# Summing pairs of tap products by an accumulating DMA ahead of TensorE's transposes

## The chip, the cores and the metric

The kernel runs on one NeuronCore of a Trainium2 chip. The metric is the time of one execution on the device, in microseconds (us). A ratio given below is the mean time of one kernel's fast runs over that of the other's fast runs of the same rounds, so it is not quite the ratio of the medians quoted beside it.

## The reference

A dynamic convolution (softmax over seven tap weights per token and head, then a weighted sum of seven shifted rows) feeds a two-layer product with `h - tanh(h)` between the layers.

```
w = exp(weight_gen - max); w = w / (sum(w) + 1e-9)        # (8, 4096, 8 heads, 7 taps)
conv[s, h, :] = sum_k w[s, h, k] * x_pad[s + k, h, :]     # 192 channels = 8 heads x 24
h = conv @ w_in                                           # (32768, 192) @ (192, 2048)
out = (h - tanh(h)) @ w_out                               # (32768, 2048) @ (2048, 192)
```

## The kernel before

The tokens go through in 32 superblocks of 1024. For each, GpSimd multiplies x by the weights, once per tap (seven `prod` tiles, tokens on partitions). TensorE then transposes each product by a matmul against an identity and adds the seven taps up in PSUM in the same step (`pc`): 3 chunks x 4 column blocks x 2 row halves x 7 taps = 168 small matmuls. ScalarE copies the sum to `convT`. Sixteen first products (`ph`, one per f tile of 128) follow, each read by ScalarE (`th`, tanh) and then VectorE (`gt`, the difference); the second product (`po`) of the superblock before is woven in.

```python
psum_h = ctx.enter_context(tc.tile_pool(name="psum_h", bufs=3, space=bass.MemoryType.PSUM))
# ... products(n): GpSimd, seven products, each in its own buffer (two of each)
for k in range(K):
    prod = ppool.tile([P, NC, J, H, GC], BF16, name=f"prod{k}", tag=f"prod{k}")
    eng = nc.vector if k in on_vector else nc.gpsimd
    eng.tensor_mul(prod[:]..., x_t[:, k : k + J, :]..., wsm[:, :, :, k : k + 1]...)
# ... conv(n, chunks): TensorE
pc = psum_h.tile([P, 2, HT], FP32, name="pc", tag="ph")      # shares the three ph buffers
for k in range(K):
    for ci, c in enumerate(chunks):
        for j in range(JH):
            for r in range(2):
                nc.tensor.matmul(pc[:, r, col : col + R], lhsT=prods[k][...], rhs=ident[...], ...)
# ... the main loop
for n in range(NTOT):
    if n + 2 < NTOT:
        products(n + 2)
    for p in range(J):
        gemm1(n, 2 * p)          # ph, th, gt
        gemm1(n, 2 * p + 1)
        if n >= 1:
            gemm2((n - 1) * J + p)
        if n + 1 < NTOT:
            if p == (2 if n else 5):
                conv(n + 1, (0, 1))      # "first place": 112 matmuls
            if p == (5 if n else 6):
                conv(n + 1, (2,))        # "third chunk": 56 matmuls
```

The softmax here doesn't subtract the row's maximum and nothing guards it: scores larger than these inputs give would overflow.

## Time and profile before

| | before |
|---|---|
| median of 3 runs | 821.86 us (821.55 to 822.88) |
| profiled span | 820.7 us |
| transposes of superblock 2 start | 69.1 us |
| clean superblock in the middle | 23.82 us |
| transposes of superblock 31 start | 767.3 us |

The first line of the page is where a reader starts; it gives busy time, share of the span and number of instructions of each engine:

```profile
PE 769.5 (94%) x16640; PEld 602.6 (73%) x16640; DVE 661.0 (81%) x591; ACT 640.1 (78%) x865; POOL 669.0 (82%) x265
```

It says "TensorE bound". Two lines of the waits give the engine that waited, for what, us in total, times, and the longest:

```profile
PE pc L169 <- issue: 2.6, 5, 1.0
PE po L223 <- issue: 2.4, 3, 1.9
```

These are gaps that no wait in the profile explains. They fall in some of the superblocks; the irregular ones take 24.0 to 24.5 us in the middle of the run. The transposes of superblock 2 are this row of the timeline of 24 to 72 us:

```profile
69.14 1.81 PE L169 MATMUL pc<-ident,prod 64*128 64x64 bf16 x110
```

### The profile page before, as it was taken

The page shows a single profiled execution, that of the slowest core. Times are in us where ns is not written, and L with a number is a line of the kernel's source. Part 1 is how long each engine was busy: PE and PEld are TensorE (multiplying, and loading weights), DVE is VectorE, ACT ScalarE, POOL GpSimd, SP SyncE. Part 2 cuts the span into 40 slices and gives each one's busy share as a digit, 9 for nine tenths or more (in the row PEclk, how much of TensorE's full clock was granted, in tenths as well). Part 3 has the DMA queues.
Part 4 walks back from the last instruction along what each step waited for, and adds up shares of the span by engine and source line. Part 5 has one row for each costly group of instructions (what it writes and reads, how often), then busy time and mean ns, then how long its engine had stood idle before and what let it go on. Part 6 is the DMA issues. An engine that isn't in the chain of part 4 may idle for free.

```text
span 820.7 us, 35994 instructions
## 1 busy us (share of the span) xinstructions
PE 769.5 (94%) x16640; PEld 602.6 (73%) x16640; DVE 661.0 (81%) x591; ACT 640.1 (78%) x865; POOL 669.0 (82%) x265
## 2 busy tenths in 40 slices
PE   0379999999999999999999999999999999999997
PEld 0247777777778777777777777777777878777777
DVE  3987878888888887887888888888888888787783
ACT  0277778888888878888888888888888888888883
POOL 5999999998898888899888889988888898885000
PEclk9989999999999999999999999999999999999999
DMA  8823333233224323332333332233233223301112
GB/s 145 216 80 81 119 120 119 71 119 120 96 77 119 120 70 120 102 94 95 119 102 87 120 120 73 99 119 114 76 120 110 95 87 120 108 3 42 41 41 79
DMA packets 17286, 81.21 MB, mean 99 GB/s; under 512 B 4160, under 2 KB 8816, under 8 KB 12984
## 3 DMA queue, kind: packets, MB, share of 16 engines
q1 hardware_dynamic: 14560, 77.34, 28.2%
q0 software_dynamic: 2576, 1.57, 1.7%
q8 instruction: 130, 2.13, 1.1%
q14 instruction: 20, 0.16, 0.1%
HBM read 54.49 MB, written 25.17 MB: 97 GB/s over the span
## 4 chain that ended last, share of the span: by engine, by line
PE 79%; DVE 13%; ACT 4%; issue 2%; DMA 1%; SPq 0%; POOL 0%; ACTq 0%; DVEq 0%; POOLq 0%
PE ph L192 36%; PE po L223 35%; DVE gt L203 10%; PE pc L169 6%; ACT th L201 4%; DVE prod L146 3%; DMA x_t<-in_x_dram 1%; PE po L264 1%; DVE zr L129 0%; DVE zsum L125 0%; POOL wsm L136 0%; SPq L96 0%; ACT e_t L115 0%; SPq L100 0%; SPq L77 0%
## 5 line engine op out<-in xcount | busy, mean ns | idle before, releaser
L203 DVE TENSOR_TENSOR gt<-ph,th 128x1024 bf16<-128x1024 f32 x512 | 602.5, 1219 | 130.0 <-ACT th L201 130.0
L146 POOL TENSOR_TENSOR prod<-x_t,wsm 128x1536 bf16<-128x1536 f32 x218 | 632.6, 2939 | 78.0 <-issue 70.3
L201 ACT ACTIVATE th<-ph 128x1024 f32<-128x1024 f32 x512 | 496.9, 1022 | 58.3 <-PE ph L192 56.3
L192 PE MATMUL ph<-convT,w_in 64*128 64x512 bf16 x3072 | 393.1, 378 | 13.8 <-DVE gt L203 10.5
L223 PEld LDWEIGHTS <-gt 64*128 64x128 bf16 x7936 | 346.1, 94 | 54.4 <-issue 3.4
L223 PE MATMUL po<-w_out,gt 64*128 64x192 bf16 x7936 | 375.8, 243 | 4.2 <-issue 2.4
L192 PEld LDWEIGHTS <-w_in 64*128 64x128 bf16 x3072 | 171.3, 94 | 128.5 <-issue 38.1
L169 PE MATMUL pc<-ident,prod 64*128 64x64 bf16 x5376 | 93.7, 192 | 29.4 <-POOL prod L146 25.9
L169 PEld LDWEIGHTS <-prod 64*128 64x128 bf16 x5376 | 89.8, 96 | 31.2 <-POOL prod L146 26.2
L179 ACT ACTIVATE convT<-pc 128x1024 bf16<-128x1024 f32 x64 | 51.9, 810 | 65.0 <-PE pc L169 65.0
L248 ACT ACTIVATE out_sb<-po 128x192 f32<-128x192 f32 x248 | 82.5, 333 | 24.3 <-PE po L223 20.7
L115 ACT ACTIVATE e_t<-wg_t 128x448 f32<-128x448 f32 x32 | 18.5, 577 | 20.9 <-DMA wg_t<-in_weight_gen_dram 20.9
L136 POOL TENSOR_TENSOR wsm<-e_t,zr 128x448 f32<-128x448 f32 x32 | 31.1, 972 | 1.7 <-DVE zr L129 1.7
L146 DVE TENSOR_TENSOR prod<-x_t,wsm 128x1536 bf16<-128x1536 f32 x6 | 21.0, 3556 | 10.8 <-DMA x_t<-in_x_dram 9.6
L125 DVE TENSOR_REDUCE zsum<-e_t 128x64 f32<-128x448 f32 x32 | 19.5, 609 | 2.8 <-ACT e_t L115 2.8
L129 DVE RECIPROCAL zr<-zsum 128x64 f32<-128x64 f32 x32 | 17.7, 553 | 3.4 <-DVE zsum L125 0.5
L264 PE MATMUL po<-w_out,gt 64*128 64x192 bf16 x256 | 11.0, 243 | 0.0
L264 PEld LDWEIGHTS <-gt 64*128 64x128 bf16 x256 | 10.8, 93 | 0.0
L276 DVE TENSOR_TENSOR out_sb<-po,ot 128x192 f32<-128x192 f32 x8 | 2.9, 357 | 8.9 <-ACT ot L275 8.9
L275 ACT ACTIVATE ot<-po 128x192 f32<-128x192 f32 x8 | 2.6, 330 | 7.9 <-PE po L264 7.9
L292 POOL DMA_DIRECT2D w_in<-in_moe_w_in_dram x8 | 4.8, 604 | 0.4 <-issue 0.4
L115 ACT ACT_TABLE_LOAD x1 | 1.3, 1283 | 0.7 <-PEq L346 0.7
(8 smaller groups left out, 2.4 us busy)
## 6 DMA issues: line engine op xcount, KB each, us to landing
x_t<-in_x_dram SPq DMA_DIRECT2D x24, 1344.0 KB
out_dram<-out_sb SPq DMA_DIRECT2D x31, 768.0 KB
x_t<-in_x_dram SPq DMA_DIRECT2D x8, 1176.0 KB
wg_t<-in_weight_gen_dram SPq DMA_DIRECT2D x32, 224.0 KB
x_t<-in_x_dram SPq DMA_DIRECT2D x8, 157.5 KB
w_in<-in_moe_w_in_dram POOLq DMA_DIRECT2D x8, 96.0 KB, 11.2
w_in<-w_in SPq DMA_DIRECT2D x1, 768.0 KB
w_out<-in_moe_w_out_dram POOLq DMA_DIRECT2D x1, 768.0 KB, 13.0
```

The source lines that it names most:

```text
L115: nc.scalar.activation(out=e_t[:].rearrange("p j h k -> p (j h k)"), in_=wg_t[:].rearrange("p j h k -> p (j h k)"), func=ACT.Exp,)
L125: nc.vector.reduce_sum(out=zsum[:], in_=e_t[:].rearrange("p j h k -> p (j h) k"), axis=AX.X)
L136: nc.gpsimd.tensor_mul(wsm[:].rearrange("p j h k -> p (j h) k"), e_t[:].rearrange("p j h k -> p (j h) k"), zr[:].rearrange("p (n o) -> p n ...
L146: eng.tensor_mul(prod[:].rearrange("p c j h g -> p j h c g"), x_t[:, k : k + J, :].rearrange("p j (h c g) -> p j h c g", h=H, c=NC), wsm[: ...
L169: nc.tensor.matmul(pc[:, r, col : col + R], lhsT=prods[k][r * R : (r + 1) * R, c, 2 * j : 2 * j + 2].rearrange("p j h g -> p (j h g)"), rh ...
L179: nc.scalar.activation(out=convT[:, c0 : c0 + nch, :].rearrange("p c (j r t) -> p r (c j) t", r=2, t=R), in_=pc[:, :, 0 : nch * JH * R].re ...
L192: nc.tensor.matmul(ph[:, r, :], lhsT=w_in[r * R : (r + 1) * R, c, f * P : (f + 1) * P], rhs=convT[r * R : (r + 1) * R, c, :], start=(c == ...
L201: last_act[0] = nc.scalar.activation(out=th[:], in_=ph_f, func=ACT.Tanh)
L203: nc.vector.tensor_sub(gt[:], ph_f, th[:])
L223: mm = nc.tensor.matmul(po[:, 0:D], lhsT=g_of[n][f][r * R : (r + 1) * R, col : col + P], rhs=w_out[r * R : (r + 1) * R, f, :], start=(r == ...
L248: last_act[0] = nc.scalar.activation(out=out_sb[:, j, :], in_=po[:, 0:D], func=ACT.Copy)
L264: nc.tensor.matmul(po[:, r, 0:D], lhsT=g_of[n][f][r * R : (r + 1) * R, col : col + P], rhs=w_out[r * R : (r + 1) * R, f, :], start=(f == 0 ...
```

## The change

The even taps 0, 2, 4 go into one tile, the odd taps 1, 3, 5 into another, tap 6 into a third. One DMA per superblock adds the odd tile into the even one, so that TensorE has four groups to transpose in place of seven (96 matmuls in place of 168).

```diff
-        prods = []
+        even = ppool.tile([P, NPAIR, NC, J, H, GC], BF16, name="even")
+        odd = ppool.tile([P, NPAIR, NC, J, H, GC], BF16, name="odd")
+        last = ppool.tile([P, NC, J, H, GC], BF16, name="last")
+        dst = {}          # taps 0 to 6: even, odd, even, odd, even, odd, last   (cut)
         for k in range(K):
-            prod = ppool.tile([P, NC, J, H, GC], BF16, name=f"prod{k}", tag=f"prod{k}")
             eng = nc.vector if k in on_vector else nc.gpsimd
             eng.tensor_mul(
-                prod[:].rearrange("p c j h g -> p j h c g"),
+                dst[k].rearrange("p c j h g -> p j h c g"),
                 # ... cut
             )
+            if k == K - 2:
+                nc.gpsimd.dma_start(
+                    out=even[:].rearrange("p i c j h g -> p (i c j h g)"),
+                    in_=odd[:].rearrange("p i c j h g -> p (i c j h g)"),
+                    accum_op=mybir.AluOpType.add,
+                    max_dma_last_dim=3072,
+                )
-        prods_of[n] = prods
+        prods_of[n] = [even[:, i] for i in range(NPAIR)] + [last[:]]
 # ... in conv
-        for k in range(K):
+        for k in range(NPAIR + 1):
```

More of the change, by code (lines that the diff above doesn't have):

```diff
@@ L44 @@
     GC = G // NC
+    NPAIR = K // 2
     assert S % TOK == 0 and D % R == 0 and H * GC == R and F % P == 0
@@ L140, in products @@
         )
-        prods = []
+        even = ppool.tile([P, NPAIR, NC, J, H, GC], BF16, name="even")
+        odd = ppool.tile([P, NPAIR, NC, J, H, GC], BF16, name="odd")
+        last = ppool.tile([P, NC, J, H, GC], BF16, name="last")
+        dst = {}
+        for i in range(NPAIR):
+            dst[2 * i] = even[:, i]
+            dst[2 * i + 1] = odd[:, i]
+        dst[K - 1] = last[:]
         for k in range(K):
-            prod = ppool.tile([P, NC, J, H, GC], BF16, name=f"prod{k}", tag=f"prod{k}")
             eng = nc.vector if k in on_vector else nc.gpsimd
             eng.tensor_mul(
-                prod[:].rearrange("p c j h g -> p j h c g"),
+                dst[k].rearrange("p c j h g -> p j h c g"),
                 x_t[:, k : k + J, :].rearrange("p j (h c g) -> p j h c g", h=H, c=NC),
@@ L152, in products @@
             )
-            prods.append(prod)
-        prods_of[n] = prods
+            if k == K - 2:
[6 more added lines that the diff above has]
+        prods_of[n] = [even[:, i] for i in range(NPAIR)] + [last[:]]
     def conv(n, chunks):
@@ L175, in conv @@
                             start=(k == 0 and ci == 0 and j == 0),
-                            stop=(k == K - 1 and ci == nch - 1 and j == JH - 1),
+                            stop=(k == NPAIR and ci == nch - 1 and j == JH - 1),
                         )
```

## The prediction

> **What bounds the kernel now.** I first read the table of busy shares (TensorE 94%, VectorE 81%, GpSimd 82%, ScalarE 78%) and the groups of instructions. Three groups matter in each of the 32 superblocks: the two matrix products, the transposes of the seven tap products (the `pc` rows), and the evacuation `gt`, which frees the PSUM that the first product writes.
>
> ```profile
> L203 DVE TENSOR_TENSOR gt<-ph,th 128x1024 bf16<-128x1024 f32 x512 | 602.5, 1219 | 130.0 <-ACT th L201 130.0
> L146 POOL TENSOR_TENSOR prod<-x_t,wsm 128x1536 bf16<-128x1536 f32 x218 | 632.6, 2939 | 78.0 <-issue 70.3
> L192 PE MATMUL ph<-convT,w_in 64*128 64x512 bf16 x3072 | 393.1, 378 | 13.8 <-DVE gt L203 10.5
> L169 PE MATMUL pc<-ident,prod 64*128 64x64 bf16 x5376 | 93.7, 192 | 29.4 <-POOL prod L146 25.9
> ```
>
> Read here: the transposes keep TensorE busy 93.7 us, 2.93 us a superblock. Four groups in place of seven would leave 4/7 of it, so the naive gain is 3/7 x 93.7 = 40 us, 5%. Busy time of a pipelined engine is not its pace, so I went on to the timeline, in order of time, of one superblock in the steady middle. Columns: start, length, engine and line, operation, count.
>
> ```profile
> 503.44 2.36 DVE L203 TENSOR_TENSOR gt<-ph,th 128x1024 bf16<-128x1024 f32 x2 [0.26 <-ACT th L201]
> 504.14 1.81 PE L169 MATMUL pc<-ident,prod 64*128 64x64 bf16 x112
> 505.77 1.48 PE L192 MATMUL ph<-convT,w_in 64*128 64x512 bf16 x12
> 505.99 1.02 ACT L179 ACTIVATE convT<-pc 128x1024 bf16<-128x1024 f32 x1 [1.30 <-PE pc L169]
> 507.96 4.71 DVE L203 TENSOR_TENSOR gt<-ph,th 128x1024 bf16<-128x1024 f32 x4 [0.98 <-ACT th L201]
> 508.39 1.68 PE L192 MATMUL ph<-convT,w_in 64*128 64x512 bf16 x12
> 511.20 1.48 PE L192 MATMUL ph<-convT,w_in 64*128 64x512 bf16 x12
> 513.12 2.36 DVE L203 TENSOR_TENSOR gt<-ph,th 128x1024 bf16<-128x1024 f32 x2 [0.45 <-ACT th L201]
> 513.82 1.00 PE L169 MATMUL pc<-ident,prod 64*128 64x64 bf16 x56
> 514.63 1.72 PE L192 MATMUL ph<-convT,w_in 64*128 64x512 bf16 x12
> 517.50 1.48 PE L192 MATMUL ph<-convT,w_in 64*128 64x512 bf16 x12
> 520.11 1.48 PE L192 MATMUL ph<-convT,w_in 64*128 64x512 bf16 x12
> ```
>
> A pair of f tiles without a transpose takes 520.11 - 517.50 = 2.61 us. The transposes of two chunks (112 matmuls) put in 505.77 - 504.14 = 1.63 us, those of the third (56) 514.63 - 513.82 = 0.81 us; that is 14.5 ns a matmul. Two pairs are longer than 2.61: the one from 508.39 by 0.20 and the one from 514.63 by 0.26. Their twelve matmuls last 1.68 and 1.72 us, not 1.48: a stall inside the group, too short to be counted as idle. The sum, 8 x 2.61 + 1.63 + 0.81 + 0.46 = 23.8 us, is one superblock.
>
> Where the stalls come from is in the first and the eighth row. `ph` and `pc` share three PSUM buffers. With a `pc` between two pairs, the second `ph` of the next pair gets the buffer of the second `ph` of the pair before, and must wait for its `gt`. In the row of 513.12 that `gt` ends at 513.12 + 2.36 = 515.48; the second `ph` started at 515.53 by the single instructions, though TensorE could have begun at 514.63 + 0.645 = 515.28. So around the third chunk **VectorE already sets the pace**, and around the first two TensorE does, by a little.
>
> The last views are GpSimd's timeline and the waits:
>
> ```profile
> 27.88 1.23 POOL L301 DMA_DIRECT2D w_out<-in_moe_w_out_dram  x1
> 50.30 20.06 POOL L146 TENSOR_TENSOR prod<-x_t,wsm 128x1536 bf16<-128x1536 f32 x7
> 71.36 20.06 POOL L146 TENSOR_TENSOR prod<-x_t,wsm 128x1536 bf16<-128x1536 f32 x7
> 490.43 20.06 POOL L146 TENSOR_TENSOR prod<-x_t,wsm 128x1536 bf16<-128x1536 f32 x7 [2.83 <-issue]
> 514.25 20.06 POOL L146 TENSOR_TENSOR prod<-x_t,wsm 128x1536 bf16<-128x1536 f32 x7 [2.83 <-issue]
> ```
>
> Early on GpSimd runs without a pause, 71.36 - 50.30 = 21.06 us a superblock; later it starts one every 514.25 - 490.43 = 23.82 us, and waits 2.83 us first. That wait, named "issue", ends when the third chunk (513.82, 0.81 long) has read the product buffers: GpSimd waits for TensorE, and has 2.8 us to spare.
>
> **What the Trainium skill says.** (1) "Perfetto Trace Analysis", Optimizing Tensor Performance: independent matmul groups should rotate through PSUM banks so that evacuation overlaps the next group. The trace agrees, and shows the limit, three buffers and 2.36 us of `gt` per 2.61 us pair. (2) "DMA: Bandwidth & Descriptors", Anatomy of one DMA: a DMA issued from GpSimd costs about 2 us fixed, mostly completion, beside its bytes; the trace's one comparable case, `w_out`, has 1.23 us on the engine and lands 13.0 us after issue, in the crowded start. (3) "Collectives: The Full Stack", The bandwidth ceiling: a reduce reads two sources and gets about half the rate of a copy, 32.35 GB/s on two engines. No accumulating DMA is in this trace. (4) "SBUF — State Buffer", Who interferes with whom: a VectorE instruction with two SBUF inputs contends with GpSimd, one with a single SBUF input doesn't. The trace agrees: a product took up to 4.48 us beside VectorE's products in the start and takes 2.90 us beside `gt`, which has one input in PSUM. So faster `gt` traffic should not slow GpSimd.
>
> **The change, part by part.**
>
> Removed: 3 of 7 tap groups, 72 of 168 matmuls a superblock (48 from the first place, 24 from the third chunk), 72 x 14.5 ns = 1.04 us of TensorE's pace. I work it through the row above.
> - First place. The transposes end after 64 x 14.5 ns = 0.93 us, at 505.07. The first `ph` follows; the second could start at 505.72 but must wait for the `gt` that ends at 503.44 + 2.36 = 505.80, so it starts at about 505.85, where before it was 505.77 + 0.645 = 506.42. Gain so far 0.57. The ScalarE copy starts 0.70 earlier, at 505.29, so the following `th` and `gt` move too: that `gt` starts at about 507.26 and ends 1.22 later, 508.48, and the second `ph` of the pair after starts at 508.53, where it was 509.24 (508.39 + 0.645 + 0.20). Gain 0.71 us.
> - Third chunk. The transposes end 0.35 us earlier, but the second `ph` still waits for the `gt` that ends 1.66 us after they start: again 1.71 us after. Gain 0; the stall grows from 0.26 to about 0.6 us.
>
> So a superblock goes from 23.81 to 23.10 us, two thirds of the matmul saving and little over half of the busy saving.
>
> Added on GpSimd: one DMA issue a superblock. `w_out` took 1.23 us for 2048 rows and the `w_in` parts 0.58 us for 24 each; this has 128 x 3 rows of 3 KB, so I estimate 0.8 us, and 0.2 us to see its own last product done. GpSimd: 21.06 + 1.0 = 22.1 us, under 23.1. It stays off the path in the steady part, with 1 us to spare in place of 2.8.
>
> Added to the DMA engines: 1.18 MB read twice and written once. Estimate from the Collectives page: 32.35/2 x 16 = 259 GB/s, 4.6 us, plus 2 us fixed and about 1 us of sharing with loads: **landing 7.5 us after issue**. In the steady part a product set starts when the third chunk before has been read; its issue comes 6 x 2.87 + 0.8 = 18.0 us later, landing 25.5 us after the start; it is needed 2 x 23.1 - 9.4 = 36.8 us after it. Hidden, with 11 us to spare.
>
> In the start nothing is hidden, since GpSimd is behind: the transposes of superblock 2 started at 69.1 us as its last products came out (50.30 + 20.06 = 70.4). Now: products from about 51.3 (one issue later), sixth done at 68.5, issue to 69.4, landing at about 76.9. **That is +7.8 us**, paid once, because from there TensorE's 23.1 is longer than GpSimd's 22.1. (The first superblock too waits for its DMA, some 5 us, but that lies within this delay, not on top.)
>
> Sum, from that point: 29 superblocks x 0.71 = -20.6, the last one's -0.7, the start +7.8: -13.5 us. I add +1: superblocks in the trace average 24.07 us between 69.1 and 767.3, 0.26 over the clean 23.81, much of it short TensorE "issue" waits, which I take to be late instructions; more DMA traffic may lengthen them. 821.86 - 13.5 + 1 = 809; I say 808.
>
> **The rivals.**
> - *Full gain*: TensorE is the bound as its 94% says. Then 31 x 1.04 to 1.26 us, less the start, give 790 to 797. For it: the page's chain of waits is 79% TensorE. Against it: the `gt` rows, which end 0.05 us before the stalled matmuls start.
> - *GpSimd becomes the bound*: if issue and own wait cost over 2 us, each superblock takes over 23.1; at 3 us it is 24.1, and the time about 829 + 8 of start, near 835. For it: only 2.8 us to spare before. Against it: the short issue rows.
> - *The accumulating DMA is slow*: the two sets of buffers close a loop of two superblocks. Behind GpSimd it costs nothing up to a landing of some 17 us; at 30 us it would set about 29 us a superblock, 980 us. For it: no such DMA measured here. Against it: the DMA engines are busy 30% only.
> - *The start costs less*: if the landing takes 5 us, the time is 805.
>
> **Range and chances.** Taking startup +4 to +13 us and gain 0.5 to 1.0 us a superblock gives 797 to 820. The 2% line is 805.4, close under my figure: faster 0.35. Slower by 2% needs one of the two slow rivals: 0.07. Within: 0.58.
>
> **What would show it.** Right: 3072 transposes; superblocks of 23.1 us; after the third chunk the twelve `ph` matmuls spread over more than 1.72 us, ending on `gt`; GpSimd 22.1 us in the early part, then still waiting about 1 us for buffers; first waits of the transposes on DMA `even`, the one of superblock 2 near 77 us; no such wait later. Wrong: superblocks near 22.7 (the `gt` limit gives way), product pitch of 23 us or more with no GpSimd wait, or transposes that wait for the DMA in every superblock.

## The result, and the profile after

| | before | after |
|---|---|---|
| median of 4 runs each | 822.37 us | 807.81 us (807.62 to 808.31) |
| ratio, 95% interval | | 0.9823 (0.9806 to 0.984): within 2% |
| profiled span | 820.7 us | 805.8 us |
| transposes of superblock 2 start | 69.1 us | 80.2 us |
| clean superblock in the middle | 23.82 us | 23.12 us |
| transposes of superblock 31 start | 767.3 us | 753.2 us |

The page's busy line, four groups, and the line of the issues that carries the new DMA (KB each, us from issue to landing):

```profile
PE 737.1 (91%) x14336; PEld 566.7 (70%) x14336; DVE 661.5 (82%) x591; ACT 643.4 (80%) x865; POOL 713.0 (88%) x297
...
L216 DVE TENSOR_TENSOR gt<-ph,th 128x1024 bf16<-128x1024 f32 x512 | 602.8, 1220 | 106.7 <-ACT th L214 103.3
...
L182 PE MATMUL pc<-ident,even 64*128 64x64 bf16 x2304 | 46.6, 193 | 45.9 <-DMA even<-odd 45.6
...
L161 POOL DMA_DIRECT2D even<-odd x32 | 41.5, 1298 | 10.0 <-POOL odd L153 9.4
...
L182 PE MATMUL pc<-ident,last 64*128 64x64 bf16 x768 | 23.4, 193 | 0.0
...
even<-odd POOLq DMA_DIRECT2D x32, 1152.0 KB, 10.1
```

The transposes are 3072 now, as intended, and TensorE's busy share fell to 91%. VectorE's `gt` is as it was. 45.6 us of waiting for the DMA stands in front of the transposes; the waits put it down to two occasions, 42.0 us before the first transposes of all and 3.6 us before those of superblock 2, so it is the start. The timeline of a superblock in the middle:

```profile
498.22 2.36 DVE L216 TENSOR_TENSOR gt<-ph,th 128x1024 bf16<-128x1024 f32 x2 [0.26 <-ACT th L214]
498.91 0.88 PE L182 MATMUL pc<-ident,even 64*128 64x64 bf16 x48
...
499.85 1.60 PE L205 MATMUL ph<-convT,w_in 64*128 64x512 bf16 x12
...
502.59 1.55 PE L205 MATMUL ph<-convT,w_in 64*128 64x512 bf16 x12
...
507.20 2.36 DVE L216 TENSOR_TENSOR gt<-ph,th 128x1024 bf16<-128x1024 f32 x2 [0.33 <-ACT th L214]
...
507.89 0.53 PE L182 MATMUL pc<-ident,even 64*128 64x64 bf16 x24
...
508.48 0.82 PE L205 MATMUL ph<-convT,w_in 64*128 64x512 bf16 x6
...
509.60 0.82 PE L205 MATMUL ph<-convT,w_in 64*128 64x512 bf16 x6 [0.30 <-DVE gt L216]
...
522.03 0.88 PE L182 MATMUL pc<-ident,even 64*128 64x64 bf16 x48
```

From 498.91 to 522.03 is 23.12 us. Around the third chunk the stall can now be seen as a wait: the twelve `ph` matmuls fall into two rows of six, and the second six start at 509.60, 0.04 us after the `gt` of 507.20 + 2.36 = 509.56. That is 1.71 us after the transposes began, in the kernel after as in the kernel before (515.53 - 513.82). In the first place the next pair follows sooner, and the pair of 502.59 has lost most of its stall (1.55 us for twelve, before 1.68).

The start, from the timeline of 24 to 82 us (the fifth row, a product, also ends GpSimd's cycle that began at 52.01; the last row is the transposes of superblock 2):

```profile
52.01 2.91 POOL L153 TENSOR_TENSOR even<-x_t,wsm 128x1536 bf16<-128x1536 f32 x1
...
69.52 1.30 POOL L161 DMA_DIRECT2D even<-odd  x1 [0.31 <-POOL odd L153]
70.34 3.41 POOL L153 TENSOR_TENSOR last<-x_t,wsm 128x1536 bf16<-128x1536 f32 x1
73.21 1.47 POOL L137 TENSOR_TENSOR wsm<-e_t,zr 128x448 f32<-128x448 f32 x1
74.75 2.90 POOL L153 TENSOR_TENSOR even<-x_t,wsm 128x1536 bf16<-128x1536 f32 x1
...
80.17 1.39 PE L182 MATMUL pc<-ident,even 64*128 64x64 bf16 x48 [3.62 <-DMA even<-odd]
```

GpSimd takes 74.75 - 52.01 = 22.74 us a superblock, where it took 21.06: 0.31 us until its own last product is done, 0.82 us from the issue to the next product, and some 0.5 us more because that product and `wsm` last 3.41 and 1.47 us in place of 2.90 and 0.97. The DMA issued at 69.52 landed 10.5 us after the beginning of its issue, and the transposes of superblock 2 began at 80.2.

The TensorE gaps without an explanation have nearly gone; this is the only one left:

```profile
PE ph L205 <- issue: 0.9, 1, 0.9
```

The change of the span, 805.8 - 820.7 = -14.9 us, splits into four:

| part | us |
|---|---|
| start, to the transposes of superblock 2 (69.1 to 80.2) | +11.0 |
| 29 superblocks, 23.12 in place of 23.82 clean | -20.3 |
| irregular superblocks: what the 29 took over 29 clean ones (7.4 before, 2.5 after) | -4.9 |
| from the transposes of superblock 31 to the end (53.4 to 52.7) | -0.7 |

### The profile page after: what moved, and what is told of

Its sections match the earlier page's. It is cut to its first block, busy times and chain, and to the rows that moved or that the text cites. A ratio compares the mean times of both kernels' runs of the same rounds, so it can differ in the third digit from the quotient of the medians.

```text
span 805.8 us, 31480 instructions
## 1 busy us (share of the span) xinstructions
PE 737.1 (91%) x14336; PEld 566.7 (70%) x14336; DVE 661.5 (82%) x591; ACT 643.4 (80%) x865; POOL 713.0 (88%) x297
## 4 chain that ended last, share of the span: by engine, by line
PE 76%; DVE 11%; POOL 5%; ACT 4%; DMA 3%; issue 1%; SPq 0%; POOLq 0%; DVEq 0%
PE ph L205 36%; PE po L236 35%; DVE gt L216 9%; ACT th L214 4%; PE pc L182 4%; POOL even L153 2%; POOL odd L153 2%; DMA x_t<-in_x_dram 1%; DVE odd L153 1%; PE po L277 1%; DMA even<-odd 1%; POOL last L153 0%; POOL wsm L137 0%; POOL even L161 0%; DVE even L153 0%
## 5 line engine op out<-in xcount | busy, mean ns | idle before, releaser
L216 DVE TENSOR_TENSOR gt<-ph,th 128x1024 bf16<-128x1024 f32 x512 | 602.8, 1220 | 106.7 <-ACT th L214 103.3
L153 POOL TENSOR_TENSOR even<-x_t,wsm 128x1536 bf16<-128x1536 f32 x95 | 281.8, 2967 | 14.2 <-DMA x_t<-in_x_dram 7.1
L153 POOL TENSOR_TENSOR odd<-x_t,wsm 128x1536 bf16<-128x1536 f32 x92 | 268.5, 2919 | 0.0
L153 POOL TENSOR_TENSOR last<-x_t,wsm 128x1536 bf16<-128x1536 f32 x31 | 105.9, 3415 | 0.0
L182 PE MATMUL pc<-ident,even 64*128 64x64 bf16 x2304 | 46.6, 193 | 45.9 <-DMA even<-odd 45.6
L182 PEld LDWEIGHTS <-even 64*128 64x128 bf16 x2304 | 43.7, 97 | 46.7 <-issue 46.4
L161 POOL DMA_DIRECT2D even<-odd x32 | 41.5, 1298 | 10.0 <-POOL odd L153 9.4
L137 POOL TENSOR_TENSOR wsm<-e_t,zr 128x448 f32<-128x448 f32 x32 | 46.3, 1446 | 0.0
L116 ACT ACTIVATE e_t<-wg_t 128x448 f32<-128x448 f32 x32 | 18.5, 578 | 20.3 <-DMA wg_t<-in_weight_gen_dram 20.3
L182 PE MATMUL pc<-ident,last 64*128 64x64 bf16 x768 | 23.4, 193 | 0.0
L153 DVE TENSOR_TENSOR odd<-x_t,wsm 128x1536 bf16<-128x1536 f32 x4 | 15.0, 3782 | 9.6 <-DMA x_t<-in_x_dram 9.6
L182 PEld LDWEIGHTS <-last 64*128 64x128 bf16 x768 | 17.3, 97 | 0.0
## 6 DMA issues: line engine op xcount, KB each, us to landing
even<-odd POOLq DMA_DIRECT2D x32, 1152.0 KB, 10.1
```

Of the source, the lines that this page charges most:

```text
L137: nc.gpsimd.tensor_mul(wsm[:].rearrange("p j h k -> p (j h) k"), e_t[:].rearrange("p j h k -> p (j h) k"), zr[:].rearrange("p (n o) -> p n ...
L153: eng.tensor_mul(dst[k].rearrange("p c j h g -> p j h c g"), x_t[:, k : k + J, :].rearrange("p j (h c g) -> p j h c g", h=H, c=NC), wsm[:, ...
L161: nc.gpsimd.dma_start(out=even[:].rearrange("p i c j h g -> p (i c j h g)"), in_=odd[:].rearrange("p i c j h g -> p (i c j h g)"), accum_o ...
L182: nc.tensor.matmul(pc[:, r, col : col + R], lhsT=prods[k][r * R : (r + 1) * R, c, 2 * j : 2 * j + 2].rearrange("p j h g -> p (j h g)"), rh ...
L216: nc.vector.tensor_sub(gt[:], ph_f, th[:])
```

## The experiments

My theory had two parts. The gain of a superblock is capped because the second `ph` after a `pc` waits for a `gt`; and the DMA costs time in the start alone. The rivals: TensorE's own pace sets the superblock, GpSimd has become the bound, or the DMA's traffic slows the other engines. In what follows the length of a superblock is the distance from the start of its first transposes to that of the next superblock's in the trace. An edit is against the changed kernel where nothing else is said; what only follows from it (a tile allocated, the `stop` flag of the last group) is cut from the diffs.

### 1. Four groups, no DMA (result wrong)

```diff
-            if k == K - 2:
-                nc.gpsimd.dma_start(out=even..., in_=odd..., accum_op=add, ...)
```

> Wrong result on purpose: only the accumulating DMA is taken out, the even taps and the last one are still transposed as four groups. My theory (the gain of a superblock is capped by the wait of the second ph for gt, and the DMA costs only in the start): a superblock still takes 23.1 us, the transposes of superblock 2 start near 69 us as in the kernel before instead of 80.2 us, and the time is 795 to 799. Rival, the DMA's traffic slows the steady part: superblocks of 22.7 us or less, 786 or less. Rival, the DMA costs nothing anywhere: 807.

Measured: 796.0 us, ratio 0.968 (0.9653 to 0.9707). Clean superblocks of 23.11 us, transposes of superblock 2 at 68.9 us:

```profile
68.92 0.94 PE L175 MATMUL pc<-ident,even 64*128 64x64 bf16 x48
```

The span is 794.5 us, 11.3 less than with the DMA, and the start is 80.2 - 68.9 = 11.3 us earlier. So the DMA costs 11.3 us, all of it before superblock 2, and nothing in the steady part. It also shows that GpSimd (21.06 us here) is not what holds the superblock at 23.1.

### 2. Seven groups and the DMA

The sum goes to a scratch tile that nobody reads; the result is right.

```diff
-                    out=even[:].rearrange("p i c j h g -> p (i c j h g)"),
+                    out=scratch[:],
-        prods_of[n] = [even[:, i] for i in range(NPAIR)] + [last[:]]
+        prods_of[n] = [dst[k] for k in range(K)]
```

> Right result: the buffers and the accumulating DMA of the changed kernel, but its sum goes into a scratch tile that nothing reads, and all seven groups are transposed. My theory: GpSimd needs 22.7 us and TensorE 23.8, so the DMA hides: superblocks of 23.8 us, no transposes waiting for the DMA, time 821 to 826 (a few us for GpSimd's later start). Rival, the DMA traffic slows other engines: superblocks of 24.3 us or more, 835 or more. It also tells whether the late TensorE instructions of the kernel before (waits named issue in the transposes) go away because of the DMA or because there are fewer matmuls: they stay if it is the matmuls.

Measured: 842.68 us, ratio 1.0247 (1.0223 to 1.0271), well above what I expected. Clean superblocks do take 23.82 us, but few are clean: the mean is 24.71 us. TensorE's waits:

```profile
PE po L238 <- issue: 9.7, 10, 2.2
PE pc L184 <- issue: 3.5, 7, 0.7
PE pc L184 <- POOL last L155: 2.6, 1, 2.6
PE ph L207 <- issue: 2.1, 4, 1.0
```

The gaps named "issue" come to 15.3 us. The first two superblocks after superblock 2 also take 27.5 and 27.7 us (before: 24.1 and 26.0), while GpSimd, slower by the DMA's issue, has no lead. So my second part was too simple: the same DMA that costs the four-group kernel nothing in the steady part costs the seven-group kernel some 20 us. (This run also has its products in three tiles in place of seven. The first run of section 7 takes superblocks 2 and 3 with seven groups from these three tiles and without the DMA; they take 24.3 and 25.7 us there, much as in the kernel before, so the tiles alone don't do it.) Put side by side, the TensorE waits named "issue":

| | no DMA | DMA |
|---|---|---|
| seven groups | 5.3 us (before) | 15.3 us |
| four groups | 1.1 us | 0.9 us (after) |

With four groups these gaps are fewer, and with seven groups the DMA makes them worse; why it does stays open. They are not gone for good: the four-group kernels of sections 6 and 7, which also have the DMA, show 4.3 us of them (two issues), and 3.0 and 4.4 us (late start with three and with five superblocks; 1.9 of the 4.4 while it still transposes seven groups). Each total is that of one traced execution.

What they are: the page's instruction queue moves 130 packets in the kernels with seven groups and 112 in those with four, each of 16,384 bytes. That is one for every 256 of TensorE's instructions (16,640 + 16,640 before, 14,336 + 14,336 after), so the queue carries TensorE's own instructions. In the traces of all 14 runs TensorE has 67 gaps named "issue". Each of them ends 2.2 to 2.8 us after an instruction packet has started, though such stretches fill only 10% of the time in the kernel before. Most packets bring no gap: 9 of the 130 did in the kernel before, 21 of the 130 here. That speaks strongly for instructions that come late; no run took the instruction traffic away by itself, so this is argued, not shown.

### 3. Transposes in three places of 56

```diff
-                if p == (2 if n else 5):
-                    conv(n + 1, (0, 1))
-                if p == (5 if n else 6):
-                    conv(n + 1, (2,))
+                if p == (2 if n else 5):
+                    conv(n + 1, (0,))
+                if p == (4 if n else 6):
+                    conv(n + 1, (1,))
+                if p == (6 if n else 7):
+                    conv(n + 1, (2,))
```

This is the kernel before (seven groups, no DMA) otherwise.

> Right result: the kernel before with its transposes in three places of 56 matmuls each in place of 112 and 56. It asks what makes the irregular superblocks of the kernel before (24.0 to 24.5 us, some with a TensorE gap of 0.5 to 1.2 us in the 112 transposes that no wait explains). If they come from the long burst of short matmuls, which uses instructions up faster than they come: no gap named issue over 0.3 us in the transposes, superblocks even; each of them 8 x 2.61 + 3 x 1.07 = 24.1 us, because every place costs at least the wait for gt. If they come from the DMA traffic alone: as many gaps as before, 2.5 us or more in transposes.

Measured: 825.97 us (one execution). GpSimd's product sets follow each other at 24.11 us once it has to wait, evenly but for one of 25.05 us, where a gap falls, and one of 24.40 us near the end, and the gaps named "issue" are 1.1 us in the transposes (one) and 0.7 in `po` (one), 1.8 in place of 5.3. The 24.1 us confirm that each place costs about 1.07 us more than its pair, the wait for `gt`, though 56 transposes need only 0.81. That no gap over 0.3 us would be left in the transposes was wrong by one. With the 112-long burst broken up the gaps are fewer, by these two traces, of which this one is a single execution. Even so the third place costs more than the gaps.

### 4. `gt` without `th` (result wrong), a failed test

```diff
-        nc.vector.tensor_sub(gt[:], ph_f, th[:])
+        nc.vector.tensor_sub(gt[:], ph_f, fixed[:])
```

It was run on the kernel before, on the changed one and on the four groups without the DMA, one execution each.

> Wrong result on purpose: in the kernel before, gt subtracts a fixed tile of zeros, so that it no longer waits for th and frees the ph buffer about 1 us sooner; busy times stay. My theory (the second ph of a pair waits for gt after each place of transposes): the two stalls of 0.20 and 0.26 us go, a superblock takes 8 x 2.61 + 1.63 + 0.81 = 23.35 us in place of 23.82, the time is 805 to 811. Rival, TensorE's own pace is the bound and the longer groups come from switching between kinds of matmuls: superblocks of 23.8 us, 820 or more.

> Wrong result on purpose: the same in the changed kernel. My theory: TensorE alone would take 8 x 2.61 + 0.92 + 0.46 = 22.3 us, but GpSimd now needs 22.74, so a superblock takes 22.7 us and the transposes wait for the DMA or the products in most superblocks: 795 to 800. Rival, TensorE's own pace: 23.1 us, 806 or more.

> Wrong result on purpose: the same without the DMA, so that GpSimd needs only 21.1 us. My theory: superblocks of 22.3 us, that is the full saving of the matmuls against the 23.35 of the kernel before with the same cut: 772 to 778. Rival, GpSimd was not the limit of the run with the DMA: the same superblock as there.

Measured: 824.37, 812.78 and 798.64 us, superblocks of 23.88, 23.18 and 23.18 us. By my expectations the rival would have won. But the waits of the second run show that the edit did not do what it was for:

```profile
DVE gt L218 <- ACT th L216: 109.4, 248, 4.1
```

`gt` still waits for `th`, 109.4 us, as much as before the edit (103.3). Both read the same `ph`. The Trainium skill, "PSUM — Partial Sum Buffer", section PSUM bank collisions raise a hardware error, says that any two engines on one bank and quadrant must be kept apart, two readers too; the trace agrees as far as it goes, the wait being there without the data to pass. So these runs tell nothing about the theory.

### 5. `th` without `ph` (result wrong)

Here ScalarE's tanh reads a fixed tile in SBUF, so that `ph` has one reader. (The order that the kernel takes from `th` for its first second-product now comes from `gt`.)

```diff
-        last_act[0] = nc.scalar.activation(out=th[:], in_=ph_f, func=ACT.Tanh)
+        nc.scalar.activation(out=th[:], in_=fixed[:], func=ACT.Tanh)
-        nc.vector.tensor_sub(gt[:], ph_f, th[:])
+        last_act[0] = nc.vector.tensor_sub(gt[:], ph_f, th[:])
```

> Wrong result on purpose: in the kernel before, ScalarE's tanh reads a fixed SBUF tile in place of ph, so that gt no longer waits for a ScalarE read of the same PSUM and follows the matmuls directly; numbers and kinds of instructions stay. My theory (the second ph of a pair waits for gt after each place of transposes): the stalls of 0.20 and 0.26 us go, a superblock takes 8 x 2.61 + 1.63 + 0.81 = 23.3 us in place of 23.82. Rival, TensorE's own pace makes the longer groups: 23.8 us.

> Wrong result on purpose: the same in the changed kernel. My theory: TensorE alone would take 8 x 2.61 + 0.92 + 0.46 = 22.3 us, but GpSimd needs 22.74, so a superblock goes from 23.12 to 22.7 us and transposes wait for the DMA. Rival, TensorE's own pace: it stays at 23.1 us.

> Wrong result on purpose: the same without the DMA, so that GpSimd needs only 21.1 us. My theory: superblocks of 22.3 us, so that three groups fewer are worth the whole 1.04 us of their matmuls when gt does not cap it. Rival, TensorE's own pace: 23.1 us.

Measured: 815.06, 798.87 and 786.07 us (one execution each); clean superblocks of 23.60, 22.75 and 22.75 us. Each fell, by 0.22, 0.37 and 0.36 us, with TensorE's instructions unchanged; its own pace was not the bound. The size was off, and the changed kernel's timeline with this edit says why:

```profile
516.20 2.36 DVE L218 TENSOR_TENSOR gt<-ph,th 128x1024 bf16<-128x1024 f32 x2 [0.26 <-ACT th L216]
517.29 0.88 PE L184 MATMUL pc<-ident,even 64*128 64x64 bf16 x48
...
526.30 0.53 PE L184 MATMUL pc<-ident,even 64*128 64x64 bf16 x24
...
526.77 1.68 PE L207 MATMUL ph<-convT,w_in 64*128 64x512 bf16 x12
```

(The two halves are of the timeline of 512 to 518 us and of 520 to 530 us.) `gt` starts 517.29 - 516.20 = 1.09 us ahead of the transposes where it started 498.91 - 498.22 = 0.69 ahead: 0.40 us earlier, not the full 1 us, since `th` still has its turn on ScalarE, behind a copy that waits for `po`. With `gt` 0.40 us sooner the second `ph` may start 1.71 - 0.40 = 1.31 us after the third chunk's transposes begin; TensorE would need 0.46 + 0.645 = 1.11. A stall of 0.20 us should be left, and the twelve matmuls take 1.68 in place of 1.48. The single instructions agree: that `gt` ends at 527.57, and the second `ph` starts at 527.62, 1.32 us after the transposes. The wait for `gt` is thus shown as the cap, in direction and in size. That the third run equals the second also shows that GpSimd, at 22.74 us, was not what held the second at 22.75; that they came so close was chance.

### 6. The DMA issued in two parts

```diff
-                nc.gpsimd.dma_start(out=even[:]..., in_=odd[:]..., ...)
+                for q0, q1 in ((0, 2), (2, 3)):
+                    nc.gpsimd.dma_start(out=even[:, q0:q1]..., in_=odd[:, q0:q1]..., ...)
```

> Right result: the accumulating DMA is issued as two, pairs 0 and 1 and then pair 2, with the same bytes. My theory: GpSimd has only 23.12 - 22.74 = 0.4 us to spare, and a second issue of 0.8 to 1.3 us makes it the bound: superblocks of 23.5 to 24.0 us, time 819 to 833. Rival, GpSimd is well off the path: superblocks of 23.1 us, time 806 to 810.

Measured: 811.74 us, ratio 0.9869 (0.9851 to 0.9887). I had the second issue too dear: GpSimd goes from 22.74 to 23.18 us, 0.44 more, not 0.8 to 1.3. TensorE's superblocks stay at 23.11. GpSimd never waits for a buffer any more and is even a little slower than TensorE: the changed kernel has 0.4 us to spare on GpSimd and no more. Of the 4.2 us lost, 2.5 us are gone by superblock 7 and 1.7 us go in two later superblocks (24.06 and 23.89 us). TensorE's gaps named "issue", 4.3 us where the changed kernel has 0.9, fall in four of the long superblocks (24.7, 24.8 and those two), so most of the loss goes with them and not with GpSimd's pace; what brings them is open, as in section 2.

### 7. The DMA only once GpSimd has a lead

The first superblocks transpose seven groups without the DMA. The result is right.

```diff
+    DIRECT = 5
-            if k == K - 2:
+            if k == K - 2 and n >= DIRECT:
-        prods_of[n] = [even[:, i] for i in range(NPAIR)] + [last[:]]
+        prods_of[n] = (
+            [dst[k] for k in range(K)]
+            if n < DIRECT
+            else [even[:, i] for i in range(NPAIR)] + [last[:]]
+        )
-        for k in range(NPAIR + 1):
+        for k in range(len(prods)):
```

> Right result: superblocks 0 to 4 transpose all seven groups without the DMA, the others as in the changed kernel. My theory (the DMA's landing costs some 11 us once, while GpSimd has no lead, and GpSimd gains 2.7 us a superblock without it): transposes of superblock 2 at about 69 us, superblocks 0 to 4 at 23.8 us, the others at 23.1, no wait of transposes for the DMA over 1 us: 797 to 803. If the start is not where the time is lost: 807 to 810.

Measured: 801.53 us (800.93 to 801.95), ratio 0.9746 (0.9727 to 0.9764), where the changed kernel has 0.9823. Transposes of superblock 2 at 69.3 us; later superblocks at 23.11, once a few irregular ones have passed. Superblock 5 starts 9.1 us ahead of the changed kernel, superblock 31 still 6.0 us. **This version beats both kernels.**

With three such superblocks in place of five:

> Right result: superblocks 0 to 2 without the DMA, the others with it. My theory: GpSimd has a lead of only about 3 us when the DMA comes in, so the transposes of superblock 3 wait for its landing until about 99.5 us, 6 us later than the 93.5 of the kernel before; the start costs 6 in place of 11 us, and the time lies between the changed kernel and the one with five such superblocks: 802 to 806. If the lead of GpSimd does not matter: 800 or less.

Measured: 805.85 us, ratio 0.9829 (0.9806 to 0.9851). The transposes of superblock 3 start at 98.9 us (expected 99.5; 93.5 with five), after 5.5 us of waiting for the DMA. The time lies in the expected 802 to 806, but by the ratio this version is no better than the changed kernel (0.9823): it is 5.8 us ahead of it at superblock 3, and 4.3 of these are lost again in irregular superblocks of 23.9 to 24.9 us up to superblock 8, which my expectation did not have. The lead of GpSimd is what hides the landing: without the DMA it gains about 2.7 us a superblock, and three superblocks are too few.

## Why the prediction was right

The time, 808 against 807.81, is closer than its terms, and that is luck. The sum of the terms was 809.4; the prediction rounds it to 809 and then says 808 without a reason. Two of the terms were off in opposite directions.

- **The gain of a superblock** (predicted 23.81 to 23.10, measured 23.82 to 23.12) held. So did its working: nothing gained at the third chunk (1.71 us in both kernels), all of it in the first place. The runs of section 5 show the wait for `gt` as the cap, and the full-gain rival is out.
- **The start** had the right mechanism and too small a size: +11.0 us, not +7.8. The term that was mis-sized most is "landing 7.5 us after issue". The DMA of superblock 2 landed 10.5 us after its issue began, and the median is 10.1. The prediction counts from when GpSimd is through with the issue, 69.4; that was 70.34, and from there the landing took 9.7 us. So 2.2 us of the error are the landing and 0.9 us a later issue, 0.7 of it because the products started at 52.01 and not at 51.3 (the term of GpSimd below). Section 1 shows that this is the whole cost of the DMA.
- **The +1 us for irregular superblocks** had the wrong sign. The irregular part shrank, by 4.9 us, and the gaps named "issue" with it, from 5.3 to 0.9 us. I thought of the DMA's traffic and not of the transposes that go. Section 2 shows both effects; in the changed kernel the second one wins. This error (-5.9) outweighs that of the start (+3.2), and the two leave -2.7 us.
- **GpSimd** takes 22.74 us, not 22.1: the term "0.8 us issue and 0.2 us to see its own product done" measured 1.68 us. It still fits under 23.1, so the steady superblock did not suffer, and the spare time is 0.4 us, not 1; it made the start 0.7 us later. That GpSimd's wait in the kernel before ends when the third chunk has read the buffers was not quite right: it ends at 514.25, 0.38 us before that chunk is through (514.63).
- **The rivals**: GpSimd as the bound and the slow DMA did not come about, though both were nearer than I gave them. (The sum for GpSimd as the bound, 829 + 8, gives 837 and not 835.) The steady landing is needed 36.8 us after the product set starts and comes 17.5 + 10 = 27 us after it by these rows.

## What to carry to other kernels

Before counting a saving on the busiest engine, find which wait ends last at the place where the work is removed: here a third of the matmul time, all of it at the third chunk, was already covered by a wait for a PSUM buffer. Work moved to a DMA is free only while its producer runs ahead of its consumer by more than the landing time, so bring it in after that lead exists. An experiment that cuts a dependency should be checked in its own trace first: section 4 cut the data and left the wait.

## What the Trainium skill lacked or had wrong

- "DMA: Bandwidth & Descriptors" has no landing time for an accumulating DMA. Here 1152 KB from SBUF into SBUF land 10.1 us (median) after issue, where my estimate gave 7.5, from the rate in "Collectives: The Full Stack", 2 us of fixed cost and 1 us of sharing.
- The same page (Anatomy of one DMA) calls descriptor generation small and variable. Here one issue a superblock lengthens GpSimd's cycle by 1.68 us (21.06 to 22.74; 0.82 us from the issue to the next product), and a second one, right behind it, by 0.44 more.
- "Runtime: NRT & Kernel Launch", Instruction fetch mechanics, says that the refill of instructions in blocks of 16 KiB is mostly hidden. The packets here have that size, and "mostly" holds: 9 of 130 are followed by a TensorE gap named "issue" in the kernel before, 5.3 us in all. With seven groups and the DMA it is 21 of 130, 15.3 us; the page doesn't say when the refill shows. That the gaps are late instructions is argued in section 2, not shown.
